# A gated linear attention and a low-rank mixer on one core: first unit's log sums in two tiles, last first-batch unit in halves with its scan ahead of a weight join, seven stores in two parts

## The chip, the cores and the metric

The kernel runs on one core of a Trainium2 chip. It uses all of that core's engines: TensorE (PE in the profile; its weight loads are PEld), VectorE (DVE), ScalarE (ACT), GpSimd (POOL) and SyncE (SP), whose queue issues nearly all DMAs. The metric is the device time of one execution in microseconds (us); the number of a kernel is the median of its runs. The profile is one further execution, with every instruction's start and duration.

## What is computed

Inputs are float32 for the attention (`q`, `k`, `v`, `f_logit`, each 4 x 8 x 768 x 48) and float64 for the mixer's weights (`U` 768 x 32, `V` 32 x 768, `w_ch1` 384 x 1536, `w_ch2` 1536 x 384). Cut to what matters:

```
f = sigmoid(f_logit)
for t in range(S):                                  # S = 768, per batch and head
    state = f[t][:, None] * state + outer(k[t], v[t])
    y[t] = q[t] @ state
x = y laid out as (B, S, H * D)                      # 4 x 768 x 384
u = x + ((x.T @ U) @ V).T                            # mixing over the 768 positions, rank 32
out = u + relu(u @ w_ch1) @ w_ch2
```

## The kernel before, in words

**Units and batches.** The attention is cut into 16 units: 4 batches of 4 pairs of heads. A pair fills 128 partitions (two heads padded to 64). Time is cut into 12 chunks of 64 positions, `NCH`, or 6 blocks of 128, `NBL`. A unit has a front (`prepare`, L754) and a rear (`attend`, L935). Units 0 to 3 are the first batch. In their front, `logs` (L798) takes the logarithm of the gates, `log_sums` (L813) sums it within each chunk by six products with a triangular matrix into a two-bank PSUM tile, and `keep_logs` (L822) lets ACT take exponentials of these sums: `X` (L830), `Y` (L831), the whole decay of each chunk (`least`, L832), and a copy of it (L835). `keys` and `queries` turn k and q on TensorE (L771) and multiply them by X and Y on DVE (L785). In the rear, `kept` (L973) turns the keys back (L980) and ACT copies them (L984), `spread` (L988) repeats the decays (L990), `states` (L992) makes each chunk's outer products (L1001) and ACT copies them to `added` (L1008), `scan` (L1013) runs one DVE scan over 48 columns x 12 chunks (L1023), `scores` and `mask` make the products within chunks (L953, L966), `read` (L1029) reads the states (L1039; ACT's tiny L1046 follows), and `inner` (L1048) adds the products within chunks (L1057), which ACT copies into x (L1063).

**Weights.** A float64 weight is loaded raw, and turned into float32 in two steps of `weight_loader` (L60): `halves`, two ACT instructions (L91, L92) into the scratch tiles `w_y` (two buffers) and `w_r` (three buffers), and `join`, three DVE instructions (L98, L99, L100) and an integer addition on POOL (L101). `weights[0]` is U, `weights[1]` and `weights[2]` are the two pieces of V (the second has 64 partitions and serves the last two of six blocks), then come twelve pieces of w_ch1 and twelve of w_ch2. A w_ch1 piece early on uses the same two `w_y` buffers as V's pieces.

**Mixer.** `low_rank_of` (L242; L184, L248) and `added_up_of` (L250; L252, L253) make `h` from x and U; `mix_of` (L255) multiplies by V (L268) and adds to x through `add` (L201, L204); `turn` transposes u (L288, L289); `ch1` (L294, L300) ends in a ReLU on ACT (L335). For the first batch `ch2` (L345, L352) makes the second layer, adds x into an output tile `o` (three buffers) and calls `store` (L339). Later batches use `seven` (L392, products at L386), Strassen-like products over quarters of w_ch2, and the last five of twelve row pairs also `fewer` (L443, L489). In `seven`, the left half of `o0` is final after step 0; step 1 uses the right half for a passing value; step 2 stores `o1`; step 3 writes the right half and stores `o0`.

**Order.** TensorE's order is the program's order in the whole kernel. That of DVE and ACT is too until the first batch's mixer is through (the `with` of L1153), and SP's up to L1226. Afterwards a planner orders these engines, by priorities and its own model of the times. The change touches the loop over `n in range(HP)` (L1187). Its last pass, `last` (n = 3), makes the list of pieces at L1190 to L1200; `join[2:]` is V's second piece, and `held` (L1183) issues loads into places that ACT frees (L1178). Behind the loop, L1227 to L1246 put the joins of the first two w_ch1 pieces (`loads[early]`, `loads[early + 1]`) among the pieces of the mixer, so on DVE they stand ahead of the additions into x.

Of the kernel before, what the change touches and what calls it, by code (L numbers as in the profile page):

```python
# [10 lines left out]
F32 = mybir.dt.float32  # L11
# [3 lines left out]
AF = mybir.ActivationFunctionType  # L15
ALU = mybir.AluOpType
# [140 lines left out]
class Mixer:  # L157
# [6 lines left out]
    def __init__(self, tc, b, x, U, V, w1, w2, sums, ident, blocks, out, two, three, zp, ps_big, ps_mm, wide=False,  # L164
                 z_all=None, room=None, pair=0):
        nc = tc.nc
        P = nc.NUM_PARTITIONS
# [33 lines left out]
        def add(*args):  # L201

            with tc.high_priority(offset=AHEAD):
                nc.vector.tensor_tensor(*args)  # L204
# [131 lines left out]

        self.some = low_rank_of, added_up_of, mix_of, turn_of, ch1_of

        def store(t, o):  # L339
            nc.sync.dma_start(out=out[b, t * P : (t + 1) * P, :], in_=o)  # L340

        po = {}
        NQ = 4
# [30 lines left out]
        W = {}  # L374
# [16 lines left out]

        def seven(a, step, parts=(0, 1)):  # L392
            x0, x1 = x[:, 2 * a, :], x[:, 2 * a + 1, :]
            if step == 0:
                pm = products(a, parts, (part(a, 0, 0), w2[:, 0:NI, lo]), (part(a, 0, 1), w2[:, NI:NFC, lo]))
                if pm is None:
                    return
                s = W["s"] = two.tile([P, WP], U32, name="w_y").bitcast(F32)
                o = W["o0"] = three.tile([P, DM], F32, name="o")
                nc.scalar.copy(s[:, hi], pm[:, lo])  # L400
                add(s[:, lo], x0[:, lo], pm[:, lo], ALU.add)
                add(o[:, lo], s[:, lo], pm[:, hi], ALU.add)
            elif step == 1:
                pm = products(a, parts, (S[a, 2], sums[2]), (S[a, 3], sums[3]))
                if pm is None:
                    return
                s, o = W["s"], W["o0"]
                add(s[:, hi], s[:, hi], pm[:, lo], ALU.add)
                add(o[:, hi], s[:, hi], pm[:, hi], ALU.add)
                o1 = W["o1"] = three.tile([P, DM], F32, name="o")  # L410
                add(o1.rearrange("p (n d) -> p n d", n=2), x1.rearrange("p (n d) -> p n d", n=2),
                    o[:, hi].unsqueeze(1).broadcast_to((P, 2, HM)), ALU.add)
                add(s[:, hi], s[:, hi], x0[:, hi], ALU.add)
            elif step == 2:
                pm = products(a, parts, (part(a, 1, 1), sums[4]), (S[a, 1], sums[1]))
                if pm is None:
                    return
                add(W["o1"], W["o1"], pm[:, 0:DM], ALU.add)
                store(2 * a + 1, W["o1"])
                add(W["s"][:, hi], W["s"][:, hi], pm[:, hi], ALU.add)  # L420
            else:
                pm = products(a, (0,), (S[a, 4], w2[:, NI:NFC, hi]))
                add(W["o0"][:, hi], W["s"][:, hi], pm[:, lo], ALU.add)
                store(2 * a, W["o0"])

        sums_x, values = {}, {}
        FG = NFC // 3
# [131 lines left out]
def factored_path(ctx, tc, q, k, v, f_logit, moe_U, moe_V, moe_w_ch1, moe_w_ch2, out, ok):  # L559
# [194 lines left out]
    def prepare(n):  # L754
# [56 lines left out]
                nc.scalar.activation(fn, fn, AF.Ln, bias=1.0)  # L811

        def log_sums():  # L813
            pt = T["sums"] = ps_big.tile([P, 2, 512], F32, name="pt", tag="big")
            for c in range(NBL):
                o = c % (NBL // 2) * (P + 2)
                nc.tensor.matmul(  # L817
                    pt[:, 2 * c // NBL, o : o + P + 2],
                    lhsT=nat[n % 2]["f"][:, c].rearrange("p h d -> p (h d)"), rhs=later, start=True, stop=True,
                )  # L820

        def keep_logs():  # L822
            by_block = T["sums"][:, :, 0 : NBL // 2 * (P + 2)].rearrange("p a (c t) -> p a c t", t=P + 2)

            def blocks_of(t):
                return t.rearrange("p (a c t) -> p a c t", a=2, t=P)

            T["X"], T["Y"] = late[:, 4 + n % 2, :], fz[n % 2][:, 0:S]
            for a in (slice(0, 1), slice(1, 2)) if n == 0 else (slice(0, 2),):
                nc.scalar.activation(blocks_of(T["X"])[:, a], by_block[:, a, :, 0:P], AF.Exp, scale=-1.0)  # L830
            nc.scalar.activation(blocks_of(T["Y"]), by_block[:, :, :, 0:P], AF.Exp)  # L831
            nc.scalar.activation(  # L832
                least[:, n, :].rearrange("p (a c s) -> p a c s", a=2, s=2), by_block[:, :, :, P : P + 2], AF.Exp, scale=-1.0
            )
            nc.scalar.copy(wholes[n % 2][:, 1:NCH], least[:, n, 1:NCH])  # L835

        def gates():
# [97 lines left out]
    def attend(n):  # L935
# [52 lines left out]
        def spread():  # L988
            whole = T["whole"] = one.tile([P, D, NCH], F32, name="whole")
            nc.scalar.copy(whole, wholes[n % 2].unsqueeze(1).broadcast_to((P, D, NCH)))  # L990

        def states():  # L992

            M = D if b else PAD
            ds = ps_big.tile([P, 2, 512], F32, name="ds", tag="big")
            for c in range(NBL):
                for s in range(2):
                    for par in range(2):

                        i = (c + (s & par)) % NBL  # L1000
                        nc.tensor.matmul(  # L1001
                            ds[par * PAD : par * PAD + M, s, c * D : (c + 1) * D],
                            lhsT=T["kb"][part[s ^ par], par, i, 0:M], rhs=vt[part[s ^ par], c, par, :],
                            start=True, stop=True,
                        )

            for r in rows if b else [slice(0, P)]:
                nc.scalar.copy(  # L1008
                    added[r, 1:].rearrange("p (e c s) -> p e c s", c=NBL, s=2),
                    ds[r, :, 0 : NBL * D].rearrange("p s (c e) -> p e c s", e=D),  # L1010
                )

        def scan():  # L1013

            st = T["st"] = two.tile([P, NCH, D], F32, name="st")
            by_e = "p (e c) -> p c e"
            if b == 0:
                states = st.rearrange("p c e -> p (c e)")
                T["st"] = states.rearrange(by_e, c=NCH)
            else:  # L1020
                states = added[:, 0 : D * NCH]
            with tc.high_priority(offset=AHEAD):
                nc.vector.tensor_tensor_scan(  # L1023
                    states, added[:, 0 : D * NCH], T["whole"].rearrange("p e c -> p (e c)"), 0.0, ALU.add, ALU.mult
                )
                if b:
                    nc.gpsimd.tensor_copy(st, states.rearrange(by_e, c=NCH))  # L1027

# [124 lines left out]
    with tc.manual_schedule(engines={nc.vector.engine, nc.scalar.engine}):  # L1153
# [33 lines left out]
        for n in range(HP):  # L1187
# [7 lines left out]
            if n == 0:  # L1195
                pieces += [lambda: busy(1, P)] + front(1, "gates", "gates_end") + rear(0, "scores", "mask")
                pieces += front(1, "unpack_k") + rear(0, "states")
            elif last:
                pieces += join[1:2] + halves[2:] + rear(n - 1, "inner") + rear(n, "states")
                pieces += join[2:] + rear(n, "scan") + [held] + rear(n, "scores", "mask")  # L1200
            else:
                pieces += front(n + 1, "gates_end", "unpack_k", "unpack_q") + rear(n - 1, "inner") + rear(n, "states")
            if n + 2 == HP:
# [461 lines left out]
```

## Time and profile before

| | us |
|---|---|
| median of 5 runs (lowest to highest) | 468.13 (467.65 to 469.73) |
| the profiled execution | 470.67 |
| its span, from the first to the last instruction | 468.9 |
| PE busy | 456.6 (97%) |
| DVE busy | 352.5 (75%) |
| ACT busy | 165.9 (35%) |
| POOL busy | 54.3 (12%) |

The page gives, for each engine, the time with an instruction in it. The chain of waits follows the work back from the last instruction, each time to what released it; 79% of it is PE, 10% DVE and 3% ACT. The timeline lists instructions by start, duration, engine, line, operation, and tiles written and read; in square brackets stands how long the engine had been idle and what ended that. A table by windows gives each engine's busy time in a stretch, then PE's granted clock (1.00 is full speed) and the DMA engines' busy share. SPq lines are issues of DMAs, with the time that the issue took; SP issues 24 stores from L340, whose data land 2.0 us later in the median.

Three stages matter below. Up to about 51 us the first batch's attention and the begin of its mixer run, where TensorE waits now and then. From there to about 300 us it is nearly always busy. From 345 to 465 us its busy time is 119.4 of 120 us. Its last product ends at 464.6, and the last store is issued at 464.98.

### The profile page before, as it was taken

The page shows a single profiled execution, that of the slowest core. Times are in us where ns is not written, and L with a number is a line of the kernel's source. Part 1 is how long each engine was busy: PE and PEld are TensorE (multiplying, and loading weights), DVE is VectorE, ACT ScalarE, POOL GpSimd, SP SyncE. Part 2 cuts the span into 40 slices and gives each one's busy share as a digit, 9 for nine tenths or more (in the row PEclk, how much of TensorE's full clock was granted, in tenths as well). Part 3 has the DMA queues.
Part 4 walks back from the last instruction along what each step waited for, and adds up shares of the span by engine and source line. Part 5 has one row for each costly group of instructions (what it writes and reads, how often), then busy time and mean ns, then how long its engine had stood idle before and what let it go on. Part 6 is the DMA issues. An engine that isn't in the chain of part 4 may idle for free.

```text
span 468.9 us, 13015 instructions
## 1 busy us (share of the span) xinstructions
PE 456.6 (97%) x5639; PEld 396.2 (84%) x5639; DVE 352.5 (75%) x581; ACT 165.9 (35%) x316; POOL 54.3 (12%) x60
## 2 busy tenths in 40 slices
PE   7989999999999999999999999999999999999996
PEld 5876888876666578899898888889989999999996
DVE  6759688988999688757675569977897887858642
ACT  6756776554332133522231323431322311212200
POOL 2003345544110100100010000120000000000000
PEclk9989999999999999999999999999999999999999
DMA  9928996768867704504533120100000000001001
GB/s 192 188 66 234 228 213 160 170 121 115 121 107 120 126 17 54 77 1 86 75 55 61 34 52 2 28 3 21 18 1 1 35 1 25 10 1 36 0 36 38
DMA packets 148344, 34.35 MB, mean 73 GB/s; under 512 B 136823, under 2 KB 146743, under 8 KB 148279
## 3 DMA queue, kind: packets, MB, share of 16 engines
q1 hardware_dynamic: 147478, 33.29, 36.8%
q8 instruction: 46, 0.75, 0.7%
q10 hardware_dynamic: 800, 0.15, 0.2%
q14 instruction: 20, 0.16, 0.1%
HBM read 28.70 MB, written 4.72 MB: 71 GB/s over the span
## 4 chain that ended last, share of the span: by engine, by line
PE 79%; DVE 10%; issue 3%; ACT 3%; DMA 2%; SPq 1%; POOL 1%; DVEq 0%; ACTq 0%; POOLq 0%
PE pw L386 25%; PE pz L300 20%; PE pp L489 12%; PE po L352 5%; PE y L1039 2%; DMA v_nat<-in_v_dram 2%; PE y L1057 2%; PE sc L953 2%; PE pt L817 2%; PE ds L1001 2%; PE pt L771 2%; PE pt L980 1%; DVE kz L748 1%; DVE late L907 1%; PE put L288 1%
## 5 line engine op out<-in xcount | busy, mean ns | idle before, releaser
L300 PE MATMUL pz<-uT,w 128*128 128x256 f32 x492 | 111.5, 382 | 0.3
L300 PEld LDWEIGHTS pz<-uT,w 128*128 128x128 f32 x492 | 91.7, 190 | 12.9 <-ACT uT L289 0.6
L1027 POOL COPY st<-added 128x576 f32<-128x576 f32 x12 | 18.2, 1515 | 187.5 <-DVE added L1023 187.5
L386 PE MATMUL pw<-zw,w_raw 128*128 128x192 f32 x216 | 38.0, 329 | 0.0
L386 PE MATMUL pw<-w,z_all 128*128 128x192 f32 x216 | 37.3, 327 | 0.0
L101 POOL TENSOR_TENSOR w<-w_y,w_r 128x384 int32<-128x384 int32 x24 | 31.5, 1314 | 39.5 <-DVE w_y L100 25.0
L386 PEld LDWEIGHTS pw<-w,z_all 128*128 128x128 f32 x216 | 35.3, 190 | 0.5
L386 PEld LDWEIGHTS pw<-zw,w_raw 128*128 128x128 f32 x216 | 35.1, 190 | 0.6 <-issue 0.3
L335 ACT ACTIVATE z_all<-pz 128x512 f32<-128x512 f32 x33 | 19.6, 597 | 45.0 <-PE pz L300 44.5
L854 DVE TENSOR_TENSOR_SCAN late<-fz,late 128x768 f32<-128x768 f32 x12 | 21.1, 1755 | 7.3 <-ACT fz L849 7.1
L482 ACT ACTIVATE other<-other 128x512 f32<-128x512 f32 x18 | 11.3, 631 | 40.3 <-DVE other L204 40.3
L352 PE MATMUL po<-w,zw 128*128 128x384 f32 x72 | 25.2, 495 | 0.0
L352 PE MATMUL po<-w,z_all 128*128 128x384 f32 x72 | 24.7, 493 | 0.0
L966 DVE TENSOR_TENSOR A<-sc,causal 128x768 f32<-128x768 f32 x16 | 15.2, 952 | 10.5 <-PE sc L953 10.5
L872 DVE TENSOR_TENSOR_SCAN late<-fz,other 128x768 f32<-128x768 f32 x12 | 22.0, 1834 | 0.2
L352 PEld LDWEIGHTS po<-w,zw 128*128 128x128 f32 x72 | 13.2, 190 | 9.6 <-issue 0.8
L352 PEld LDWEIGHTS po<-w,z_all 128*128 128x128 f32 x72 | 13.3, 190 | 8.9 <-DVE o L204 0.6
L1008 ACT COPY added<-ds 48x576 f32<-48x576 f32 (+1 forms) x28 | 17.8, 635 | 5.6 <-PE ds L1001 5.2
L482 ACT ACTIVATE z_all<-z_all 128x512 f32<-128x512 f32 x12 | 7.6, 630 | 34.1 <-DVE z_all L204 34.1
L489 PE MATMUL pp<-v_nat,late 128*128 128x128 f32 x152 | 19.1, 275 | 0.0
L1039 PEld LDWEIGHTS y<-st,qT 48*64 48x64 f32 x704 | 13.5, 137 | 6.4 <-issue 3.7
L98 DVE TENSOR_SCALAR w_y<-w_y 128x384 f32<-128x384 f32 (+3 forms) x27 | 12.1, 448 | 8.9 <-ACT w_y L91 8.9
(226 smaller groups left out, 869.9 us busy)
## 6 DMA issues: line engine op xcount, KB each, us to landing
w_raw<-in_moe_w_ch_dram SPq DMA_DIRECT2D x18, 384.0 KB, 3.7
out_dram<-o SPq DMA_DIRECT2D x24, 192.0 KB, 2.0
v_nat<-in_v_dram SPq DMA_DIRECT2D x16, 144.0 KB, 4.0
v_nat<-in_v_dram SPq DMA_DIRECT2D x32, 72.0 KB, 3.6
zw<-in_moe_w_ch_dram SPq DMA_DIRECT2D x6, 384.0 KB, 4.5
w<-in_k_dram SPq DMA_DIRECT2D x4, 288.0 KB, 4.1
w<-in_q_dram SPq DMA_DIRECT2D x4, 288.0 KB, 4.6
late<-in_f_logit_dram SPq DMA_DIRECT2D x10, 96.0 KB, 2.8
```

Of the source, the lines that this page charges most:

```text
L101: nc.gpsimd.tensor_tensor(dst.bitcast(I32), shaped(y.bitcast(I32)), shaped(r), ALU.add)
L300: nc.tensor.matmul(pm[:, i * 2 * P : (i + 1) * 2 * P], lhsT=w1[:, m, o : o + P], rhs=uT[a][:, m, :], start=(m == 0), stop=(m == NDC - 1))
L335: nc.scalar.activation(z[a, c][:, k : k + 2, :].rearrange("p i t -> p (i t)"), pm, AF.Relu)
L352: nc.tensor.matmul(pm, lhsT=z[a, i // NI][:, i % NI, s * P : (s + 1) * P], rhs=w2[:, i, :], start=(i == 0), stop=(i == NFC - 1))
L386: nc.tensor.matmul(W["pm"][:, n * HM : (n + 1) * HM], lhsT=lhs[:, i, :], rhs=rhs[:, i, :], start=(i == 0), stop=(i == NI - 1))
L482: nc.scalar.activation(dst, dst, AF.Relu, scale=float(SIGNS[n]))
L489: nc.tensor.matmul(pm[:, i, r * P : (r + 1) * P], lhsT=room["w"](wn)[:, r * P : (r + 1) * P], rhs=x_node(a, xn), start=((xn, wn) == of[0]) ...
L854: nc.vector.tensor_tensor_scan(backwards(X, S - 1, S), backwards(f, S, S), backwards(ends, S - 1, S), 0.0, ALU.mult, ALU.add,)
L872: nc.vector.tensor_tensor_scan(Y, f[:, 0:S], starts, 0.0, ALU.mult, ALU.add)
L1008: nc.scalar.copy(added[r, 1:].rearrange("p (e c s) -> p e c s", c=NBL, s=2), ds[r, :, 0 : NBL * D].rearrange("p s (c e) -> p e c s", e=D),)
L1027: nc.gpsimd.tensor_copy(st, states.rearrange(by_e, c=NCH))
L1039: nc.tensor.matmul(o(c % 2, par, c // 2), lhsT=T["q"][rows[par], chunk[c]], rhs=T["st"][rows[par], c, :], start=(c <= 2), stop=False, skip ...
```

## The change

1. `log_sums` of unit 0 writes blocks 0 to 2 to a tile of the pool `ps_mm` and blocks 3 to 5 to the second bank of the tile of before. `keep_logs` of unit 0 makes each of X, Y and `least` in two instructions, one per tile, where before only X was.
2. In the last first-batch unit (n = 3), `states` copies 24 of the 48 columns at a time, and `scan` scans 24 at a time.
3. In that unit's list, `join[2:]` moves from ahead of the scan to behind the mask.
4. `store` in batch 0 (six stores) sends rows 0 to 63 and 64 to 127 in two DMAs. In the last row pair of the last batch, the left half of `o0`'s columns is sent in step 2, behind `o1`, and step 3 sends the right half alone.

```diff
-        def store(t, o):
-            nc.sync.dma_start(out=out[b, t * P : (t + 1) * P, :], in_=o)
+        def store(t, o, cols=slice(0, DM)):
+            n = 1 if b else 2
+            for r in range(n):
+                g = slice(r * P // n, (r + 1) * P // n)
+                nc.sync.dma_start(out=out[b, t * P + g.start : t * P + g.stop, cols], in_=o[g, cols])
...
+            last_of_all = b == out.shape[0] - 1 and a == NA - 1
...
                 add(W["s"][:, hi], W["s"][:, hi], pm[:, hi], ALU.add)
+                if last_of_all:
+                    store(2 * a, W["o0"], lo)
             else:
                 pm = products(a, (0,), (S[a, 4], w2[:, NI:NFC, hi]))
                 add(W["o0"][:, hi], W["s"][:, hi], pm[:, lo], ALU.add)
-                store(2 * a, W["o0"])
+                store(2 * a, W["o0"], hi if last_of_all else slice(0, DM))
...
         def log_sums():
-            pt = T["sums"] = ps_big.tile([P, 2, 512], F32, name="pt", tag="big")
+            both = ps_big.tile([P, 2, 512], F32, name="pt", tag="big")
+            T["both"] = both
+            pt = T["sums"] = [both[:, 0:1], both[:, 1:2]]
+            if n == 0:
+                pt[0] = ps_mm.tile([P, 512], F32, name="pt0", tag="mm").unsqueeze(1)
             for c in range(NBL):
                 o = c % (NBL // 2) * (P + 2)
                 nc.tensor.matmul(
-                    pt[:, 2 * c // NBL, o : o + P + 2],
+                    pt[2 * c // NBL][:, 0, o : o + P + 2],
...
-            for a in (slice(0, 1), slice(1, 2)) if n == 0 else (slice(0, 2),):
-                nc.scalar.activation(blocks_of(T["X"])[:, a], by_block[:, a, :, 0:P], AF.Exp, scale=-1.0)
-            nc.scalar.activation(blocks_of(T["Y"]), by_block[:, :, :, 0:P], AF.Exp)
-            nc.scalar.activation(
-                least[:, n, :].rearrange("p (a c s) -> p a c s", a=2, s=2), by_block[:, :, :, P : P + 2], AF.Exp, scale=-1.0
-            )
+            of_least = least[:, n, :].rearrange("p (a c s) -> p a c s", a=2, s=2)
+            if n == 0:
+                parts = [(slice(a, a + 1), t) for a, t in enumerate(T["sums"])]
+            else:
+                parts = [(slice(0, 2), T["both"])]
+            parts = [(a, t[:, :, 0 : NBL // 2 * (P + 2)].rearrange("p a (c t) -> p a c t", t=P + 2)) for a, t in parts]
+            for a, sums in parts:
+                nc.scalar.activation(blocks_of(T["X"])[:, a], sums[:, :, :, 0:P], AF.Exp, scale=-1.0)
+            for a, sums in parts:
+                nc.scalar.activation(blocks_of(T["Y"])[:, a], sums[:, :, :, 0:P], AF.Exp)
+            for a, sums in parts:
+                nc.scalar.activation(of_least[:, a], sums[:, :, :, P : P + 2], AF.Exp, scale=-1.0)
             nc.scalar.copy(wholes[n % 2][:, 1:NCH], least[:, n, 1:NCH])
...
+        def halves_of(n):
+            return [slice(0, D // 2), slice(D // 2, D)] if n == HP - 1 else [slice(0, D)]
...
             for r in rows if b else [slice(0, P)]:
-                nc.scalar.copy(
-                    added[r, 1:].rearrange("p (e c s) -> p e c s", c=NBL, s=2),
-                    ds[r, :, 0 : NBL * D].rearrange("p s (c e) -> p e c s", e=D),
-                )
+                for e in halves_of(n):
+                    nc.scalar.copy(
+                        added[r, 1:].rearrange("p (e c s) -> p e c s", c=NBL, s=2)[:, e],
+                        ds[r, :, 0 : NBL * D].rearrange("p s (c e) -> p e c s", e=D)[:, e],
+                    )
...
-                nc.vector.tensor_tensor_scan(
-                    states, added[:, 0 : D * NCH], T["whole"].rearrange("p e c -> p (e c)"), 0.0, ALU.add, ALU.mult
-                )
+                for e in halves_of(n):
+                    of = slice(e.start * NCH, e.stop * NCH)
+                    nc.vector.tensor_tensor_scan(
+                        states[:, of], added[:, of], T["whole"].rearrange("p e c -> p (e c)")[:, of], 0.0, ALU.add, ALU.mult
+                    )
...
-                pieces += join[2:] + rear(n, "scan") + [held] + rear(n, "scores", "mask")
+                pieces += rear(n, "scan") + [held] + rear(n, "scores", "mask") + join[2:]
```

More of the change, by code (lines that the diff above doesn't have):

```diff
@@ L822, in keep_logs @@
         def keep_logs():
-            by_block = T["sums"][:, :, 0 : NBL // 2 * (P + 2)].rearrange("p a (c t) -> p a c t", t=P + 2)
             def blocks_of(t):
```

## The prediction

> **What bounds the kernel now.** I read the page's busy shares first, then the chain that ended last, then the timeline around each edited line, then the tail's DMA.
>
> ```profile
> PE 456.6 (97%) x5639; PEld 396.2 (84%) x5639; DVE 352.5 (75%) x581; ACT 165.9 (35%) x316; POOL 54.3 (12%) x60
> ```
>
> TensorE is busy 97% of the span, and its order is written by hand. So after about 46 us a delay simply travels to the end, and only three places of this change can move the end: the start (to 12 us), the last first-batch unit (37 to 47 us) and the tail. The seven edited stores elsewhere hang on SP. Timeline of the start:
>
> ```profile
> 5.32 1.76 PE L817 MATMUL pt<-later,late 128*128 128x130 f32 x12 [0.55 <-issue]
> ...
> 5.64 0.44 ACT L806 ACTIVATE late<-late 128x288 f32<-128x288 f32 x1
> ...
> 7.11 0.87 ACT L830 ACTIVATE late<-pt 128x384 f32<-128x384 f32 x2 [1.03 <-PE pt L817]
> ...
> 7.87 0.82 ACT L831 ACTIVATE fz<-pt 128x768 f32<-128x768 f32 x1
> ...
> 8.56 0.20 ACT L832 ACTIVATE least<-pt 128x12 f32<-128x12 f32 x1
> 8.79 0.20 ACT L835 COPY whole<-least 128x11 f32<-128x11 f32 x1
> ```
>
> Read it so: ACT has nothing left at 6.08 and waits until the last of the log sums is in, though its first exponential reads only the first half of them. From 7.11 to 11.85 the chain of waits is ACT work almost without a break.
>
> Timeline of the last first-batch unit:
>
> ```profile
> 37.96 0.64 ACT L1008 COPY added<-ds 128x576 f32<-128x576 f32 x1
> ...
> 38.50 0.45 POOL L101 TENSOR_TENSOR V<-w_y,w_r 64x128 int32<-64x128 int32 x1 [0.54 <-DVE w_y L100]
> ...
> 38.64 1.53 DVE L1023 TENSOR_TENSOR_SCAN st<-added,whole 128x576 f32<-128x576 f32 x1 [0.28 <-ACT added L1008]
> ...
> 40.09 0.93 DVE L966 TENSOR_TENSOR A<-sc,causal 128x768 f32<-128x768 f32 x1
> ...
> 40.32 1.23 PE L1039 MATMUL y<-st,qT 48*64 48x48 f32 x44 [0.84 <-DVE st L1023]
> ...
> 41.66 0.57 ACT L91 ACTIVATE w_y<-zw 128x384 f32<-128x384 f32 x1
> ...
> 42.65 1.04 DVE L99 TENSOR_SCALAR w_y<-w_y 128x384 uint32<-128x384 uint32 x1
> ...
> 44.20 2.08 DVE L204 TENSOR_TENSOR x<-x,pu 128x576 f32<-128x576 f32 x3
> ```
>
> TensorE waits 0.84 us for the scan. But DVE has no pause from 38.64 to 46.27 (44.20 + 2.08), and the products of L268 at 45.75 take buffers that the second and third of these additions free: the second ends at 45.61. DVE is level with TensorE there.
>
> **Part 1, log sums in two tiles.** Blocks 0 to 2 are in at about 6.2 us, so the first L830 (0.49) runs in the wait. The second still waits for 7.11; what follows it in ACT's order is longer: two L831 of 384 at the L830 pace (7.11 to 7.87 for two, 0.38 each) for one of 0.69 (7.87 to 8.56), +0.07, and a second L832, about +0.11 (what a short activation behind another takes at 106.78 to 106.89). Gain 0.38 − 0.07 − 0.11 = 0.20, about **−0.18** with the rounding. Beside it, k's product (L785, 8.02) moves only to the end of its transposes, 7.79, and is no tighter. L990, the copy of kb and the next unit's L804 follow one another on ACT. From both sides: −0.38 if the extra instructions hide, 0 if the transfers of the first 15 us (DMA share 1.00 in that window) gate unit 1 instead. I take −0.18: the next unit's f is in before DVE starts on it, at 9.76 without a wait.
>
> **Part 2, halves and the moved join.** No row shows a copy or scan of 288. By a straight line through the scans of 576 (1.356) and 768 (1.755), 2.08 ns an element and 0.16 fixed, a half scan is 0.76; ACT's 128x288 copies (L248, L253) are 0.40 and 0.37. First copy 37.96 to 38.37, first scan from 38.41, the second 0.68 behind it, done at 39.85 instead of 40.17. That includes the 0.18 by which POOL's addition at 38.50 now lengthens this scan (1.534 against 1.356). TensorE's reading gains **0.32**.
>
> The price: the three DVE instructions of the second V piece (37.27, 37.52, 38.07) ran while DVE had nothing to do. Now DVE idles from 37.36 to 38.41, and they stand behind the mask. Following the queue: mask 39.77, L98 at 40.62, L99 40.87, L100 41.13, POOL's addition 41.55 to 42.01. Two things wait. ACT's L91 at 41.66 takes the scratch tile w_y, which has two buffers, and the second V piece holds one until POOL is done: 42.04, +0.39, and ACT's copy of h (L253) behind it feeds L268. And the next two joins and the first addition into x queue on DVE. An L99 beside POOL waits it out (0.23 at 36.80 alone, 1.04 at 42.65 next to POOL's 1.05), so the first w1 join's L99 ends at 42.23, its POOL addition runs 42.96 to 44.01, the second's L99 ends at 44.23, its L100 starts at 44.27 and the first addition at 44.74 instead of 44.20. The three additions keep their 0.66 pitch, the third ends at 46.82, and L268's second tile starts that much later: **+0.55**, the scan's gain already spent. Ends: −0.32, if DVE and ACT are not what TensorE waits for; +0.80, the join's whole 0.72 and more POOL waiting. I take +0.55, since both the second and the third addition end within 0.1 us of their readers' start.
>
> SP sees `held` at the same place in its own order; its loads wait for ACT's L1178, later by 0.08. V's second piece is read at 44.23, after 42.01.
>
> **Part 3, first-batch stores in halves.** Six more issues on SP of 0.36 to 0.47 plus 0.05 between. The first (119.51) is in a full stretch, but SP then has a wait from 124.20 to 124.73; behind those at 128.12 and 141.11 it waits 2.2 and 1.3 us. Cost 0; at most one issue that finds no pause, +0.41. If all six were bare, 2.5. Three output buffers serve a store each, so nobody waits for the landing.
>
> ```profile
> v_nat<-in_v_dram SPq DMA_DIRECT2D x16, 144.0 KB, 4.0
> v_nat<-in_v_dram SPq DMA_DIRECT2D x32, 72.0 KB, 3.6
> ```
>
> The row of 64-partition loads shows half the bytes taking nine tenths of the time. The Trainium skill, "SBUF — State Buffer", section "Door 1: The DMA port swizzle", speaks against this edit: partitions 0 to 63 reach only 8 of the 16 ports, so each half would move at half rate. By that rule a split store takes as long twice, some 1.1 us for 0.53 of packets; the sum is the same by rule and row, as long as nobody waits for it.
>
> **Part 4, the last store.** The tail's DMA over 462 to 469, 0.175 us a digit:
>
> ```profile
> DMA  0000004000019981000001998530000000000000
> ```
>
> The first burst is the odd block's store, the second (465.7 on) the last store, issued at 464.98 after the addition at 464.60; the span ends 2.4 us behind it. Both move 192 KB, at 351 and 360 GB/s in the full slices: 0.54 us. With half of the columns sent early, 96 KB remain: −0.27 if bytes set the pace, 0 if packets do, whose number (one a row) stays. I take **−0.25**: the page's loads of 64 B against 128 B packets (2.9 and 2.8 us) speak for packets, but those are far smaller than 768 B. The early half goes out behind the odd block's store of 463.23, one issue of 0.33, and SP is free again near 464.0.
>
> **Sum.** −0.18 + 0.55 + 0 − 0.25 = **+0.12 us**. Durations come from one execution of 470.67 us (span 468.9, 1.77 around it), 2.54 over the median of the runs shown, 468.13. I put the sum on the median: 468.25, say **468.2 us**. A measurement of this kernel can tell about 0.3%, 1.4 us, from no change; this is far inside.
>
> **Rivals.**
>
> *A, slower: a stretch at half clock.* The windows:
>
> ```profile
> 24.59:28.00 3.41, 1.78 (x76) 1.51 (x76) 1.69 (x3) 1.72 (x3) 0.00 (x0) 1.00 0.45 106
> 28.00:31.42 3.42, 3.42 (x58) 3.33 (x51) 1.36 (x1) 1.81 (x4) 0.00 (x0) 0.50 0.04 9
> 31.42:34.83 3.41, 3.40 (x103) 2.85 (x102) 2.02 (x4) 2.50 (x7) 0.00 (x0) 1.00 0.02 5
> 38.25:41.66 3.41, 2.57 (x87) 1.89 (x78) 3.09 (x5) 1.85 (x8) 0.45 (x1) 1.00 0.53 152
> ```
>
> The first number is the stretch, the second PE's busy time, the seventh the granted clock. After a stretch with PE busy 1.78 of 3.41 the clock is 0.50 for 3.42 us; after one with 2.57 it stays 1.00. By my queue PE now idles 0.77 us before L268 (42.70 to 43.47) and 0.16 before its second tile, some 2.48 busy: just below the row that kept the clock. Should the V piece come half a microsecond later still, 2.0 is left, and nearer to 1.78. It decides somewhere between 2.57 and 1.78. Price 3.42 × 0.5 = 1.71: 468.13 + 0.12 + 1.71 = 470.0. The Trainium skill, "TensorE: Matmul & The Clock Gate", section "What's actually happening", lets the clock fall only after at least one idle window of about 3.4 us. By it this rival costs 0. The row contradicts it: the longest pause in the stretch before the half clock is the 1.63 us of "issue" at 25.86 in the chain.
>
> *B, faster: the stretch at 28.00 is not granted at half clock, and the moved join is hidden.* Everything there arrives 0.18 earlier, so the stretch that ends at 28.00 holds more work. L817 takes 2.68 in it (29.18) against 1.61 at 18.39: −1.07. With the scan's −0.32, the start's −0.18 and the tail's −0.25: −1.82, 466.3; with the join eating the scan's gain, −1.50, 466.6. Against it: the pause itself moves along.
>
> *C: the join is hidden, the clock as before.* L268 waits neither for ACT's h nor for DVE: −0.32 − 0.18 − 0.25 = −0.75, 467.4. For it: V's second piece is read late. Against it: 45.61 and 46.27 on DVE next to 45.72 and 46.33 on TensorE.
>
> *D: it doesn't do what it says.* The waits go by whole tiles: the first exponential still waits for all log sums, and the last addition into `o` waits until the early half of the store has landed, 463.6 + 2.0 instead of 464.60: +1.0. Then +0.55 + 1.0 − 0.25 = +1.3, 469.4. Against it: DVE's first L802 (3.71) began while the second half of its tile was still on its way (the second waited to 4.82).
>
> **How the numbers follow.** Forecast 0.43, C 0.20, D 0.05: all within 0.3%, 0.68. B 0.17, faster; A 0.15, slower. The unknown costs span −0.38 − 0.32 − 0.27 (467.2) to +0.80 + 0.41 (469.3). The range reaches to A's 470.0 and to B's nearer end, 466.6.
>
> **What would show it.** Right: the first L830 near 6.25, L804 of unit 1 near 10.26; two scans of about 0.76 and L1039 about 0.3 us earlier against the copy L1008; POOL's second V piece behind the mask, ACT's L91 waiting for POOL, and DVE's three additions into x some 0.55 later against L1008; the last burst of DMA half as long. Wrong: L268 starting earlier against L1008 (C), a clock of 0.50 elsewhere than at 28 to 31.4 (A, B), the last addition waiting for a DMA (D), or DVE and ACT in another order after the first batch, where the planner and not the code orders them: I priced that at nothing.

## The result, and the profile after

Changed kernel: median 467.56 us over 48 runs, kernel before on the same chips 468.3 over 91. The ratio, into which long executions enter, is 0.9976, 95% interval 0.9967 to 0.9985: 1.1 us less (0.7 to 1.5). The medians are 0.74 apart: 10 of the 91 executions of the kernel before took 470 us or more (up to 474.2) and none of the 48 of the changed kernel (a repeat of it has one, 471.03 with a mean TensorE clock of 0.989), and without those ten the means differ by 0.8. The forecast was 468.2, no change.

The profiled execution took 467.55 us (span 465.8), 3.1 less than that of before. The page of the changed kernel, TensorE's line:

```profile
PE 455.8 (98%) x5639; PEld 394.9 (85%) x5639; DVE 352.4 (76%) x582; ACT 166.1 (36%) x319; POOL 54.5 (12%) x60
```

**Where the 3.1 us are.** Matched product by product, TensorE is 0.23 ahead while unit 0 ends, 2.64 ahead at 32 us, 2.13 at 46 us, and between 2.1 and 2.2 up to the last product. Then the span ends another 0.94 sooner: from the last product's start to the end of the span it is 3.77 us, before 4.71. I call this stretch **the tail**. Nothing moved between 46 us and the tail: six split stores and the planner's order cost nothing there.

*The start.* Timeline of the changed kernel; L844 is X (before L830), L846 Y, L848 `least`, L810 the next unit's gates (before L804):

```profile
5.99 0.49 ACT L844 ACTIVATE late<-pt 128x384 f32<-128x384 f32 x1 [0.22 <-PE pt L827]
...
6.79 0.49 ACT L844 ACTIVATE late<-pt 128x384 f32<-128x384 f32 x1 [0.31 <-PE pt L827]
...
7.18 0.87 ACT L846 ACTIVATE fz<-pt 128x384 f32<-128x384 f32 x2
...
7.92 0.26 ACT L848 ACTIVATE least<-pt 128x6 f32<-128x6 f32 x2
...
10.21 0.69 ACT L810 ACTIVATE other<-other 128x576 f32<-128x576 f32 x1
```

The kernel before:

```profile
10.44 0.69 ACT L804 ACTIVATE other<-other 128x576 f32<-128x576 f32 x1
```

The first exponential runs before the second half of the sums is in; the next unit's gates start at 10.21 (before 10.44).

*The middle.* The windows of the two stretches that stood out before:

```profile
24.59:28.00 3.41, 2.34 (x105) 2.09 (x102) 1.52 (x3) 2.30 (x4) 0.00 (x0) 1.00 0.44 108
28.00:31.42 3.42, 3.42 (x87) 3.03 (x90) 2.51 (x3) 3.04 (x9) 0.00 (x0) 1.00 0.04 10
```

TensorE is busy 2.34 us of the first stretch instead of 1.78, and the next keeps its clock of 1.00. That, with shorter pauses ahead of it, is most of the 2.64; whether the change did it is tested below.

*The last first-batch unit.* L1026 is the copy to `added`, L1043 the scan, L1059 the reading:

```profile
35.40 0.70 ACT L1026 COPY added<-ds 128x288 f32<-128x288 f32 x2
35.83 1.41 DVE L1043 TENSOR_TENSOR_SCAN st<-added,whole 128x288 f32<-128x288 f32 x2 [1.04 <-ACT added L1026]
...
37.38 0.73 PE L1059 MATMUL y<-st,qT 48*64 48x48 f32 x24 [0.47 <-DVE st L1043]
...
38.52 0.72 PE L1059 MATMUL y<-st,qT 48*64 48x48 f32 x20 [0.41 <-issue]
...
38.93 0.45 POOL L101 TENSOR_TENSOR V<-w_y,w_r 64x128 int32<-64x128 int32 x1 [3.54 <-DVE w_y L100]
...
39.41 0.55 ACT L91 ACTIVATE w_y<-zw 128x384 f32<-128x384 f32 x1
...
40.86 0.77 PE L268 MATMUL pu<-h,V 32*128 32x288 f32 x8
...
42.06 2.07 DVE L204 TENSOR_TENSOR x<-x,pu 128x576 f32<-128x576 f32 x3
```

V's product in the kernel before:

```profile
43.11 0.77 PE L268 MATMUL pu<-h,V 32*128 32x288 f32 x8
```

Count from the copy (35.40, before 37.96). The reading starts at +1.98 (before +2.36), but V's product L268 at +5.46 (+5.15), and DVE's additions into x at +6.66 (+6.24). The reading is 0.38 sooner and the additions behind it are 0.42 later all the same. TensorE also stood still for 0.41 at 38.1 inside the reading.

*The tail.* DMA over 459 to 466, 0.175 us a digit; the second burst is the last store:

```profile
DMA  0000000000040000499500000039308000000000
```

It is three slices long (before five); the single 4 and 8 are packets of instructions. SyncE's waits from 461 us on, the kernel before and then the changed one (total, times, longest):

```profile
SPq L1632 <- SPq L1632: 1.6, 1, 1.6
```

```profile
SPq L1652 <- SPq L1652: 0.7, 2, 0.5
```

These lines are SyncE's closing waits for its own DMAs. Before, one wait of 1.6; now two, of 0.5 and 0.2. The semaphore records say why. (A semaphore is a counter that a DMA raises when its data have landed, and that an engine can wait for.) SyncE's DMAs take eight semaphores in rotation; at the end SyncE waits for all eight in a fixed order. Times in us from the last store's issue (in brackets the store's own semaphore):

```
before   [100] 2.042  102 2.140  104 2.221  105 2.306  106 2.377  107 2.451  108 2.517  110 2.584
changed   100  0.901  102 0.999  104 1.080  105 1.165  106 1.236  107 1.310  108 1.376 [110] 1.648
```

Before, the last store was the first of the list, and seven waits, 0.54 us, were passed after it had landed. Seven DMAs more turn the rotation by seven: the last store is now the eighth, and the seven others are passed while it is under way. It also lands after 1.65 instead of 2.04. The second effect was in my sum, too small; the first was not in it.

### The profile page after: what moved, and what is told of

The parts are those of the page before. It is cut to its first block, busy times and chain, and to the rows that moved or that the text cites. A ratio compares the mean times of both kernels' runs of the same rounds, so it can differ in the third digit from the quotient of the medians.

```text
span 465.8 us, 13023 instructions
## 1 busy us (share of the span) xinstructions
PE 455.8 (98%) x5639; PEld 394.9 (85%) x5639; DVE 352.4 (76%) x582; ACT 166.1 (36%) x319; POOL 54.5 (12%) x60
## 4 chain that ended last, share of the span: by engine, by line
PE 79%; DVE 11%; issue 3%; ACT 2%; DMA 2%; SPq 1%; POOL 1%; DVEq 0%; POOLq 0%
PE pw L389 25%; PE pz L300 21%; PE pp L495 12%; PE po L355 5%; PE y L1059 2%; PE pt L777 2%; PE y L1077 2%; PE sc L967 2%; PE ds L1018 1%; PE pt L994 1%; DVE late L868 1%; PE pt L827 1%; DVE late L921 1%; DMA w<-in_q_dram 1%; PE put L288 1%
## 5 line engine op out<-in xcount | busy, mean ns | idle before, releaser
L1026 ACT COPY added<-ds 48x576 f32<-48x576 f32 (+2 forms) x29 | 17.8, 619 | 5.1 <-PE ds L1018 4.7
L1059 PEld LDWEIGHTS y<-st,qT 48*64 48x64 f32 x704 | 13.6, 137 | 6.5 <-issue 4.5
```

The lines of the kernel that those rows point to most:

```text
L1026: nc.scalar.copy(added[r, 1:].rearrange("p (e c s) -> p e c s", c=NBL, s=2)[:, e], ds[r, :, 0 : NBL * D].rearrange("p s (c e) -> p e c s", ...
L1059: nc.tensor.matmul(o(c % 2, par, c // 2), lhsT=T["q"][rows[par], chunk[c]], rhs=T["st"][rows[par], c, :], start=(c <= 2), stop=False, skip ...
```

## Experiments

Times are medians, the experiment against the kernel before on the same chip; long executions enter the ratio more than the medians, so the two can differ. "Landing" runs from the last store's issue to SyncE passing its semaphore, "rest" is the tail without it.

| kernel | DMAs more | place in list | last store | landing | tail | rest | time / before | ratio, 95% interval |
|---|---|---|---|---|---|---|---|---|
| before | 0 | 1 | 192 KB | 2.04 | 4.71 | 2.67 | | |
| before_again | 0 | 1 | 192 KB | 2.12 | 4.79 | 2.67 | 468.16 / 468.15 | 1.0009 [0.9997, 1.0020] |
| last_store_only | 1 | 2 | 96 KB | 1.65 | 4.21 | 2.57 | 467.59 / 467.66 | 0.9995 [0.9979, 1.0011] |
| six_stores_only | 6 | 7 | 192 KB | 1.92 | 4.11 | 2.19 | 467.32 / 467.66 | 0.9985 [0.9959, 1.0011] |
| seven_more_whole | 7 | 8 | 192 KB | 2.14 | 4.27 | 2.12 | 467.46 / 467.66 | 0.9991 [0.9976, 1.0007] |
| eight_more_whole | 8 | 1 | 192 KB | 1.87 | 4.54 | 2.67 | 467.98 / 467.66 | 1.0016 [0.9990, 1.0043] |
| stores_only | 7 | 8 | 96 KB | 1.63 | 3.76 | 2.12 | 467.24 / 468.11 | 0.9986 [0.9966, 1.0006] |
| after_one_more | 8 | 1 | 96 KB | 1.63 | 4.30 | 2.67 | 467.77 / 468.11 | 1.0004 [0.9982, 1.0026] |
| changed kernel | 7 | 8 | 96 KB | 1.65 | 3.77 | 2.12 | 467.56 / 468.3 | 0.9976 [0.9967, 0.9985] |

**The tail.** *last_store_only*: the second half of part 4 alone; its main lines:

```diff
+                if last_of_all:
+                    store(2 * a, W["o0"], lo)
...
-                store(2 * a, W["o0"])
+                store(2 * a, W["o0"], hi if last_of_all else slice(0, DM))
```

> The kernel before with the last store alone in two parts (left half of the columns in step 2, right half in step 3); one DMA more in the whole kernel. My new theory of the tail: SyncE ends the kernel by waiting for its eight DMA semaphores one after another in a fixed order; the kernel before has its last store on the first of them, so that seven waits (0.54 us) stand behind its landing. One DMA more moves the last store to the second of the list, six waits stand behind it: -0.10; and the smaller store lands 0.39 sooner. From the start of the last product to the end of the span 4.70 becomes about 4.2, the time -0.5 us. The rival is my prediction's pricing, -0.25 by bytes and nothing by the order of the waits: 4.45. A second rival, that the early store's place behind the odd block's store is what shortens the tail, would give the whole -0.93 here: 3.75.

*six_stores_only*: `n = 1 if b else 2` in `store`, the last store whole.

> The kernel before with the six stores of batch 0 in two parts of 64 rows and nothing else; the last store is whole. By the theory of the semaphores, six DMAs more put the last store on the seventh of the eight in SyncE's closing list: 0.47 of the seven waits is then done while the store is under way, and one wait of 0.07 is left behind it; from the last product's start to the end of the span 4.70 becomes about 4.2, the time -0.47 us. By my prediction (cost 0, hidden in SyncE's pauses) the tail stays at 4.70 and the time at the kernel before's. If the issues of SyncE do cost somewhere in the middle, TensorE's order shows a shift after 119 us, up to +0.41.

*seven_more_whole* and *eight_more_whole*: the last store whole; of batch 0's stores the first (or the first two) in three parts, the others in two.

```diff
+            n = 1 if b else 3 if t == 0 else 2      # seven more
+            n = 1 if b else 3 if t < 2 else 2       # eight more
```

> The kernel before with seven DMAs more, all in batch 0 (its first store in three parts, the other five in two); the last store is whole, 192 KB. By the theory of the semaphores the last store is on the last of the eight in the closing list, all seven other waits are done while it is under way: the tail is 4.70 - 0.54 = 4.16, the time -0.54 us. The rival, that the number of the semaphore does not matter and the smaller last store made the whole gain of the tail, gives 4.70 and 0.

> The control: the kernel before with eight DMAs more, all in batch 0 (the first two stores in three parts, the other four in two). Eight more bring the last store back to the first semaphore of the closing list: by the theory of the semaphores the tail is again 4.70 and the time that of the kernel before, although it splits more stores than the kernel with seven more. If more and smaller stores in batch 0 help by themselves, it is as fast as that one, 4.16.

*stores_only*: all of part 4 of the change, nothing else.

> The kernel before with all seven stores split as in the changed kernel, and the start and the last first-batch unit as before. Theory: the tail is 3.77 instead of 4.70, and the middle is untouched: -0.93 us against the kernel before, as fast as the changed kernel or faster, since start (-0.2) and last first-batch unit (+0.43) together cost the changed kernel 0.2. Rival: the gain comes from the start and from shorter pauses in the first 30 us; then this kernel has the kernel before's time less 0.4.

*after_one_more*: the changed kernel with the first store in three parts.

> The changed kernel with one DMA more: batch 0's first store in three parts instead of two. Everything that shortens the last store itself is kept. Theory of the closing list: the last store goes from its last place (the eighth of the semaphores) to its first, all seven other waits stand behind its landing again: from the last product's start to the end of the span 3.77 becomes 4.3 (+0.54), the time +0.54 us against the changed kernel. Rival (the gain of the tail comes from the smaller store alone): 3.77, no difference.

Of these tails 4.21, 3.76 and 4.30 came as expected; 4.11 (for about 4.2), 4.27 (for 4.16) and 4.54 (for 4.70) differ by the landing, each taken from one profile. The column "rest" decides: it follows the place in the list and nothing else. 2.67 at the first place, with 192 or 96 KB, with no DMA more or eight; 2.12 at the last; the difference is the 0.54 of the seven waits. *more_loads* (below), with two DMAs more and the third place, has 2.49, which is 2.67 less the first two waits. The landing follows the size: 1.87 to 2.21 for 192 KB in nine profiles (mean 2.05), 1.63 to 1.65 for 96 KB in nine (mean 1.64). SyncE's line shows it as well; after_one_more has the changed kernel's small store and one wait in place of two:

```profile
SPq L1652 <- SPq L1652: 1.2, 1, 1.2
```

In time the picture is blunter: stores_only's median is 0.87 below before, as expected, but last_store_only's is only 0.07 (expected 0.5) and seven_more_whole's 0.20 (expected 0.54). Kernels whose first 35 us are the same code differ by up to 1.9 us in their profiles there (4.0 with the profile before), so single experiments of 12 runs tell half a microsecond at best. Together they tell more. The six experiments with a tail of 3.75 to 3.77 (stores_only and five of those below) have medians 0.42 to 1.21 under the kernel before on their chip, 0.80 in the mean. The four with a tail of 4.65 to 4.88 (before_again, start_only, unit_only, more_loads) lie 0.01 to 0.24 above it.

**The last first-batch unit.** *unit_only*: parts 2 and 3 of the change alone; the moved join is this line.

```diff
-                pieces += join[2:] + rear(n, "scan") + [held] + rear(n, "scores", "mask")
+                pieces += rear(n, "scan") + [held] + rear(n, "scores", "mask") + join[2:]
```

> The kernel before with the last first-batch unit's copy and scan in halves and its scan ahead of the weight join, and nothing else. Theory: the states are read 0.3 to 0.4 sooner against the copy to added, but V's product in the mixer starts 0.3 to 0.5 later against it: +0.4 us in the end, tail 4.70. My prediction said +0.55. Rival: the 0.41 of this that TensorE spent in one pause without a cause that the trace shows (at 38.12 us) is chance, then 0.

Measured 468.28 to 468.04, ratio 1.0003 [0.9980, 1.0027]. Its timeline, without a pause in the reading (L1045):

```profile
36.06 1.24 PE L1045 MATMUL y<-st,qT 48*64 48x48 f32 x44 [0.47 <-DVE st L1029]
...
38.08 0.57 ACT L91 ACTIVATE w_y<-zw 128x384 f32<-128x384 f32 x1 [0.59 <-POOL V L101]
...
39.00 0.39 ACT L253 COPY h<-ph 128x288 f32<-128x288 f32 x1
...
39.53 0.77 PE L268 MATMUL pu<-h,V 32*128 32x288 f32 x8 [0.70 <-ACT h L253]
```

ACT waits 0.59 for POOL's V piece, h is late, TensorE waits 0.70 for h. That makes L268 0.31 later; its last products, which start 0.14 to 0.15 behind the end of DVE's second addition into x in the profile before, here and in the changed kernel, are 0.43 later. From the states' products to the first MLP products this order takes 0.43 longer than the profile before, here without the pause and in the changed kernel with it: the pause only filled a wait that is there anyway. The rival falls, by the traces: the times tell nothing this small.

*after_join_ahead*: the changed kernel with `join[2:]` back ahead of the scan.

> The changed kernel with the join of V's second piece back ahead of the scan; halves, log sums and stores as in the changed kernel. Theory: the scan's gain of 0.3 is kept and the 0.4 that DVE's queue loses to the late join is not paid, so V's product starts 0.3 sooner against the copy to added than in the kernel before, 0.7 sooner than in the changed kernel: -0.7 us against the changed kernel, -1.4 against the one before. Rival: the join's POOL addition beside the first half of the scan and the three DVE instructions ahead of it delay the first half scan by as much: no better than the changed kernel.

Measured 467.62 to 468.04, ratio 0.9994 [0.9967, 1.0021]. I had expected 1.4 less than before, and the median is 0.42 less. The stretch is 0.06 shorter than in the profile before, 0.49 shorter than in the changed kernel; I had expected 0.7:

```profile
35.97 1.62 DVE L1043 TENSOR_TENSOR_SCAN st<-added,whole 128x288 f32<-128x288 f32 x2
36.08 0.90 POOL L101 TENSOR_TENSOR V<-w_y,w_r 64x128 int32<-64x128 int32 x1 [0.54 <-ACT added L1026]
...
40.62 0.77 PE L268 MATMUL pu<-h,V 32*128 32x288 f32 x8
```

The scans take 1.62 beside POOL's addition (1.41 without), so the reading gains 0.15 and not 0.3. L268 waits for nothing.

*after_whole_scan*: the changed kernel with copy and scan whole, the scan still first.

> The changed kernel with the copy to added and the scan of the last first-batch unit whole again; the scan stays ahead of the weight join. Theory: the scan is 1.36 long because POOL does not run beside it (1.53 before), so the states are read 0.18 sooner than in the kernel before, 0.2 later than in the changed kernel; the mask, the join and the additions into x queue behind it by the same 0.2: +0.2 us against the changed kernel, -0.5 against the one before. Rival: DVE's chain of additions and not the scan sets V's product, and the halves cost an instruction each: same time as the changed kernel.

Measured 467.41 to 468.04, ratio 0.9996 [0.9981, 1.0011]. The stretch takes 0.62 longer than before, 0.19 longer than in the changed kernel: the theory's 0.2. In these profiles the halves gain 0.2 where the scan goes first, and the moved join costs 0.5 with halves and 0.6 without.

**The start and the pauses.** *start_only*: part 1 alone.

> The kernel before with the log sums of unit 0 in two tiles and nothing else. Theory: unit 1's first work on TensorE and DVE comes 0.2 us sooner, and the end with it, -0.2 us; the tail stays at 4.70. Rival: pauses of TensorE between 16 and 26 us, where it waits for nothing that the trace shows, swallow it or give it back (in the profiles of before and after these pauses were 0.85 and 0.33, 1.63 and 1.07 us, and a new one of 0.24), so the time is anywhere within 0.5 us of the kernel before.

Measured 468.13 to 468.04, ratio 0.9990 [0.9958, 1.0022]. Unit 1 is 0.24 ahead of the profile before in the trace. Where the log sums end at the same time it is 0.18 ahead (start_only, after_again, join_ahead_again and after_whole_scan against six_stores_only), the predicted number. In time 0.2 us can't be seen. So the start was made worse, eightfold:

```diff
-            nc.scalar.activation(blocks_of(T["Y"]), by_block[:, :, :, 0:P], AF.Exp)
+            for _ in range(3 if n == 0 else 1):
+                nc.scalar.activation(blocks_of(T["Y"]), by_block[:, :, :, 0:P], AF.Exp)
```

> The kernel before with unit 0's exponential Y (0.82 us) done three times over, which delays ScalarE at the start by 1.64 us: the first part of the change with its sign turned and its size eightfold, to see whether a shift at the start reaches the end at all. In ten profiles TensorE paused by 0 to 1.1 us near 21 us and by 0 to 1.8 us near 27 us, each time 1.3 to 1.6 us behind the landing of a 16 KB block of the instruction queue. Theory: these blocks are asked for when TensorE gets to the one before, so the pauses move along and the whole 1.6 is found at the end: last product 1.6 us later than in profiles without a half-clock stretch (460.7 to 462.3), so 462.3 to 463.9, time +1.6. Rival: the blocks wait for the loads that fill the DMA engines up to 25 us, at fixed times; then the pauses shrink and the shift behind 28 us is below 0.8; the 0.2 us that the change gains at the start is swallowed there as well.

*start_late*: 469.32 to 468.11, ratio 1.0029 [1.0019, 1.0040]: 1.2 to 1.4 us more, with 0.9 to 1.9 in the interval. Part of that may be the clock: 8 of its 12 executions had a mean TensorE clock of 0.992 to 0.995, and 1 of 35 of the kernel before; the median of the other four is 1.0 above. Against before_again's profile the shift is 1.86 at 19 us (0.26 of it because the log sums came later there), 1.26 at 34 us and 1.28 at the end. So a shift of 1.64 reaches the end for the most part, and the rival's 0.8 is too low; how much the pauses swallow is not settled, and for a shift of 0.2 nothing is shown.

*more_loads*: two loads more behind unit 3's; the lines that issue them:

```diff
+                for t in unread:
+                    nc.sync.dma_start(out=t, in_=moe_U.rearrange("(c p) r -> p c r", p=P))
```

> The kernel before with U loaded twice more, into a buffer that nobody reads then, behind unit 3's loads: 384 KB more on the DMA engines between 23 and 26 us. It doubles a suspected cause of TensorE's pause near 27 us: the 16 KB block of instructions that it waits for shares the DMA engines with these loads. Theory: the block starts 1 us or more later than in the ten profiles shown so far (22.4 to 25.1 us), the pause ahead of the matmul that follows it grows to 1.5 us or more, and the clock is halved behind it more often; time +1 us or more. Rival: the block is late for another reason; its start stays between 22.4 and 25.1 and the time is the kernel before's.

Measured 468.12 to 468.11, ratio 1.0000 [0.9989, 1.0010]. The block started at 23.25 as ever, but the experiment missed its aim: the extra loads moved for the most part from 25 us on (127 GB/s in 25 to 26 and 178 in 27 to 28, in before_again 86 and 46), behind the block that they were to delay. The block after that one started at 27.62, and the pause behind it (0.93) is the longest at that product in 18 profiles (0.15 to 0.66 in the others), but this is one profile. What delays a block stays open.

**Repeats on one chip.** *before_again*:

> The kernel before, unchanged, for a second profile of it. Theory: the stretch at half clock at 28 us and the long pauses of TensorE ahead of it (1.07 and 1.84 us) are chance, so this profile has the last product near 461 to 462 us like the others, and the tail of 4.5 to 4.9 with seven waits behind the last store's landing. Rival: they belong to the kernel before, and the change removed them by what it does at the start; then they are here again.

Its last product starts at 461.39, 2.84 before that of the first profile (464.23), and its clock is 1.00 throughout. The half clock of the first profile belongs to that execution and not to the code: of 18 profiles, 10 of them with the old start, it alone has that stretch, and no other has longer pauses at these two places (from product start to product start 1.07, as in start_only, and 1.84). Whether the change makes such stretches rarer is not shown.

*after_again*, *stores_and_halves* (all stores split and halves, join and start as before) and *join_ahead_again*:

> The changed kernel, unchanged, for a second profile of it on the same chip as the next two. Theory: from the copy to added's product to the first products of the first MLP layer it again loses 0.43 against the kernel before, and its tail is again 3.77; whether its pause of 0.67 in the reading of the states is there or not makes no difference, since V's product waits for ScalarE's h. Time 0.7 below the kernel before. Rival: the 0.43 was the pause, and is gone when the pause is.

> The kernel before with the seven split stores and the copy and scan in halves; the weight join stays ahead of the scan and the start is as before. Theory: tail -0.93, the middle -0.06 to -0.15 (with the join ahead, the states were read 0.15 sooner in the profile shown so far), in sum -1.0 to -1.1 against the kernel before, 0.3 below the changed kernel. Rival: the changed kernel's order of the scan and the join is the better one in runs without a profile: no difference or slower.

> The changed kernel with the join of V's second piece ahead of the scan, as in after_join_ahead, now on one chip with the changed kernel and with stores_and_halves, from which it differs by the log sums in two tiles alone. Theory: 0.5 below the changed kernel, and 0.2 below stores_and_halves if the start's gain reaches the end; equal to it if the pauses up to 30 us swallow the gain.

| | median | kernel before | ratio, 95% interval |
|---|---|---|---|
| after_again | 467.54 | 468.15 | 0.9993 [0.9974, 1.0011] |
| stores_and_halves | 467.07 | 468.15 | 0.9980 [0.9968, 0.9991] |
| join_ahead_again | 466.94 | 468.15 | 0.9995 [0.9970, 1.0020] |

after_again loses the same 0.43 in the middle, and its tail is 3.77: as expected. The two kernels with the join ahead have medians 0.5 and 0.6 below it, near what was expected (their middle, with pauses of 0.67 and 0.40 in the reading that this order doesn't hide, is 0.28 and 0.20 longer than in the profile before), and stores_and_halves is faster than before beyond its interval. That they beat the changed kernel is not shown: the intervals overlap, and after_join_ahead, with the same order, had a median 0.21 above that of after_whole_scan on its chip, where its stretch is 0.68 shorter. The start's gain, the difference of the last two, can't be told from nothing.

## Why the prediction was wrong

- **Part 3, the step that failed: "Cost 0" for the six batch-0 stores.** SyncE's pauses did hide their issues: TensorE's lead over the kernel before stays at 2.1 to 2.2 us from 46 us on. (The packets of a split store run for 1.2 to 1.3 us in five of six, those of a whole one for 0.7 to 0.9 in five of six, so halves are slower, near the 1.1 I had; nobody waits for them.) But I asked only who waits for these stores, not what an extra DMA does at the end, though I had noted that the span ends 2.4 us behind the last burst: it turns the rotation of the semaphores. Six more take 0.48 out of the tail, seven 0.54 (rest 2.67 to 2.19 and to 2.12).
- **Part 4, mis-sized.** −0.25 by bytes; the landing took 0.39 less in the two profiles (2.04 to 1.65), 0.41 in the means of nine and nine. "0 if packets do" is excluded. With Part 3 the tail is −0.94 where I had −0.25.
- **Part 2, right in mechanism.** POOL's addition holds w_y, ACT's L91 waits, h and the additions into x are late. The last products of L268 do go by the additions, as I had it. I had +0.55, measured +0.43. The reading gained 0.38 (I had 0.32). But I took the profile before for typical. In ten profiles with the old order this stretch is 0 to 0.87 longer than there (mean 0.19) by pauses; with the new order it is 0.43 in four of four. So the net price is nearer 0.25 in these profiles.
- **Part 1, right in place, its arrival not shown.** Predicted −0.18; in the trace −0.23, and 0.18 where the log sums end at the same time. In the profile after, the lead is gone by 18 us, behind a pause of 0.25 at 16.4. start_late lets most of 1.64 through; no run can tell 0.2.
- **The sum** by measured terms, if the start's 0.2 arrives: −0.2 + 0.25 − 0.94 = −0.9, inside the interval of 0.7 to 1.5 less.
- **Rivals.** B's mechanism (no half clock at 28) is seen in the profile after, but in before_again too: not the change's doing. Its price was too low: between the profiles before and after, TensorE's lead grows by 1.58 over that stretch (1.06 at 28.0 us, 2.64 at 32), where B had 1.07. A did not come: no half clock behind the moved join in any of the five profiles with it. C is refuted by unit_only's 0.70 wait. Of D, the first exponential doesn't wait for all sums (5.99), and the wait of the last addition is not there: the last product's start to the store's issue is 0.75 in both.

## What to carry to other kernels

The end of a kernel is a path of its own: look at which DMA lands last, how large it is, and how many closing waits stand behind it. An edit that adds or drops a DMA anywhere can shift that order, so price it at the end as well as at its place. And before a small edit is priced from one profile, ask whether its pauses are the kernel's or that execution's.

## What the runs showed of the hardware

**The closing waits.** SyncE's walk through eight DMA semaphores costs 0.07 to 0.10 us each, after the landing or beside it, depending on a rotation that the program's number of DMAs sets.

**TensorE's pauses without a cause in the trace look like waits for instructions.** Between 15 and 51 us such a pause, where there is one, comes in each profile at the same products, some 126 apart; with their weight loads that is about 252 instructions. A 16 KB packet of the instruction queue lands 1.3 to 1.6 us ahead of the end of every such pause of 0.4 us or more in the 18 profiles (once 1.7). That TensorE waits for this packet is inferred from these times. In the table, in us, a length runs from the start of the product before the pause to the start of the one behind it, so it is 0.2 to 0.3 more than the idle time in the lines above:

```
profile            packet          pause ends  (length)
before             18.48 - 19.94     21.27      1.07
before             25.09 - 26.19     27.48      1.84
changed kernel     24.13 - 25.10     26.43      1.29
changed kernel     36.16 - 37.10     38.52      0.67
seven_more_whole   42.06 - 43.19     44.69      0.93
unit_only          22.35 - 23.27     24.99      none to speak of
```

The Trainium skill, "Runtime: NRT & Kernel Launch", section "Instruction fetch mechanics", has instructions stream in blocks of 16 KiB, 256 instructions, at a cost that is mostly hidden. The spacing agrees. The cost does not in the first 50 us, where products are short: up to 1.84 us at one block, and from 0 to 1.8 for the same code in different executions.

**The clock.** Before, a stretch of 3.41 us with TensorE busy 1.78 was followed by half the clock; the changed kernel's with 2.34 was not, and neither was one with 1.93 in start_late's profile (9.57 to 12.98 us).
